# Moving weight-conversion steps and one pair's transposes within an attention stage on one core

## The chip, the cores and the metric

The kernel runs on 1 core of one Trainium2 chip. The metric is the device time of one execution in microseconds, as the median of several runs. All data are fp32; the MLP weights come as 64-bit floats and are converted on the chip.

## What is computed

Softcapped attention, then two MLPs, for 2 batches of 448 tokens, 12 heads of 64:

```python
scores = scale * np.matmul(q, k.transpose(0, 1, 3, 2))
scores = cap * np.tanh(scores / cap)
scores = scores - np.max(scores, axis=-1, keepdims=True)
attn = np.exp(scores)
attn = attn / (np.sum(attn, axis=-1, keepdims=True) + 1e-09)
x = np.matmul(attn, v)                  # then 896 tokens x 768
r = np.maximum(x @ w_in, 0.0)           # w_in 768 x 2048
x = (s * (r * r) + b) @ w_out           # w_out 2048 x 768
h = x @ w2_in                           # 768 x 1024, then softmax-gated,
...
out = ln @ w2_out                       # normalised, and 1024 x 768
```

## The kernel before, in words

Every fp32 product with full precision is made of three matmuls, of a high and a low part each (`xh`, `xl`).

**Attention** works on 12 pairs of heads, counted from 0 (`NPR` is 12); two pairs make a group, and a group's q, k and v are loaded together (`load_group`). For a pair n: `prep` (two halves, called by `prep_half`) transposes keys and queries on TensorE (L426, tiles `pk`, `pq`) and splits them into `kh`, `kl`, `qh`, `ql` on VectorE and ScalarE (L437 to L450). `scores_by_key` makes four blocks of scores (L468) in a ring of two PSUM tiles `s`; ScalarE takes the tanh of each (L473, tile `e`). `exps_by_key` exponentiates in two halves on ScalarE (L480). `sums_by_key` adds the tiles of `e` for the denominator: half 0 is one GpSimd addition (L489), half 1 is another (L492) and then two VectorE additions (L495), all into `c`. `products_by_key` multiplies with the values on TensorE (L507, tile `o`), `values_by_key` sums `c` over the keys on TensorE (L517, tile `m`); VectorE then turns `m` (L524, `mt`), takes reciprocals (L526), turns them back (L530) and scales `o` (L535, `xf`). `split_x` makes the MLP's input from `xf`, on GpSimd (L544, L548) but for the last two pairs. The tiles `pk`, `pq`, `o` and `m` share a ring of four PSUM tiles.

**Order.** The helper `then` traces a step so that each engine issues it behind everything traced by an earlier `then` step. So the order of the calls in the loop over n (L766 on) is the order within each engine. In round n of the loop stand: scores 0 and 1 of pair n, products and values of pair n-2, the first half of the exponentials, scores 2 and 3, the second half, both halves of `prep` of pair n+2, some steps of weight conversion, and last `sums_by_key(n, 1)`. What round 0 has ahead of the loop is scores 0 and 1 of pair 0 and `prep` of pair 1.

**Weight conversion.** `Weights` holds the jobs, one for each weight block, in order: `wi0`, `wi1`, `wi2` and so on. `load` issues a block's DMA on SP's queue into one of two raw buffers (L286); a job loads the next block when it starts. `pump(n)` advances the current job by n steps. The steps of `convert` are: 1, the absolute value (L222 on VectorE for `wi0`, else L226 on ScalarE) and a clamp on VectorE (L227); 2, a shift (L231); 3, an AND and OR with the high word (L236); 4, an OR with the low word (L240), after which the raw buffer is free; 5, the copy to the high part (L247 on VectorE for `wi0`, else L249 on ScalarE) and the subtraction to the low part (L250). A sixth call closes the job. There are three places for converted blocks, so three blocks can be converted before the MLP frees one. The number of steps in each round of the attention loop is in the table `steps`, by round; rounds 12 and 13 have two each besides:

```python
steps = {1: 3, 2: 2, NPR - 2: 2, NPR - 1: 3}
```

**DMA queues.** Keys and values go over SP's queue (L112, L117). The queries of groups 0 (but for its first pair), 1 and 2 go over GpSimd's queue, those of later groups over SP's (L126).

**After attention** the first MLP's first matmuls (`in_unit`, L335 to L337) and ScalarE's relu (L353) and square follow; the conversion of further blocks is pumped between the matmuls.

Of the kernel before, what the change touches and what calls it, by code (L numbers as in the profile page):

```python
# [37 lines left out]
def tile_softcap_attention__relu2__solu(  # L38
# [15 lines left out]
    nc = tc.nc  # L54
# [67 lines left out]
    def load_by_query(t, src, b, heads, eng=None):  # L122

        for pr in range((heads.stop - heads.start) // 2):
            for j in range(2):
                (eng or nc.sync).dma_start(  # L126
                    out=t[:, pr, :, j],
                    in_=src[b, heads.start + 2 * pr + j].rearrange("(p c) d -> p c d", c=NC),
                )
# [11 lines left out]
    for pr in range(2):  # L141
# [3 lines left out]
        if pr == 0:  # L145
            for j, queue in enumerate((nc.sync, nc.scalar)):
                queue.dma_start(
                    out=first["q"][:, 0, :, j],
                    in_=q[0, j].rearrange("(p c) d -> p c d", c=NC),
# [14 lines left out]
    with psum("ps_w", 1) as ps_w:  # L164
# [4 lines left out]
        out=a_t.bitcast(U32), in0=cap_t.bitcast(U32), scalar1=0x7FFFFFFF, scalar2=None,  # L169
# [4 lines left out]
        out=sc_t, in0=r_t, scalar1=1.0 / float(D) ** 0.5, scalar2=None, op0=ALU.mult  # L174
# [7 lines left out]
    def layers(ctx, general):  # L182
# [33 lines left out]
        def convert(wt, raw, n, h, l, g=None, early=False):  # L216
            r = raw[:, :2 * n].rearrange("p (n w) -> p n w", w=2)
            lo, hi = r[:, :, 0], r[:, :, 1]
            w = wt[:, :n]
            wb = w.bitcast(U32)  # L220
            if early:
                nc.vector.tensor_scalar(  # L222
                    out=wb, in0=hi, scalar1=0x7FFFFFFF, scalar2=None, op0=ALU.bitwise_and
                )
            else:
                nc.scalar.activation(out=w, in_=hi.bitcast(F32), func=AF.Abs)  # L226
            nc.vector.tensor_scalar(  # L227
                out=w, in0=w, scalar1=LEAST, scalar2=MOST, op0=ALU.max, op1=ALU.min
            )
            yield  # L230
            nc.vector.tensor_scalar(  # L231
                out=wb, in0=wb, scalar1=3, scalar2=0x3FFFFFFF,
                op0=ALU.logical_shift_left, op1=ALU.bitwise_and,
            )
            yield
            nc.vector.scalar_tensor_tensor(  # L236
                out=wb, in0=hi, scalar=0xC0000000, in1=wb, op0=ALU.bitwise_and, op1=ALU.bitwise_or
            )
            yield
            nc.vector.scalar_tensor_tensor(  # L240
                out=wb, in0=lo, scalar=29, in1=wb,
                op0=ALU.logical_shift_right, op1=ALU.bitwise_or,
            )
            yield
            if g is None:
                if early:
                    nc.vector.tensor_copy(h, w)  # L247
                else:
                    nc.scalar.copy(out=h, in_=w)  # L249
                nc.vector.tensor_tensor(out=l, in0=w, in1=full(h), op=ALU.subtract)  # L250
            else:
                nc.scalar.mul(out=h, in_=w, mul=g)
                nc.vector.scalar_tensor_tensor(
                    out=l, in0=w, scalar=g, in1=full(h), op0=ALU.mult, op1=ALU.subtract
                )
            yield
# [128 lines left out]
        def load_group(g, names=("k", "q", "v")):  # L385
            b, i = divmod(g, GB)
            heads = slice(4 * i, 4 * i + 4)
            for nm, src in (("k", k), ("q", q), ("v", v)):
                if nm not in names:
                    continue  # L390
                by_key = nm != "q" and not general
                if g == 0 and (nm == "q" or nm == "k" and by_key):
                    nat[nm, g] = first[nm]
                    continue
                by_pair = nm != "v"
                shape = [P, 2, NC, 2, D] if by_pair else [P, 4, NC * D]
                if by_key:
                    if (nm, g % 3) not in kept:
                        kept[nm, g % 3] = ap_.tile(shape, F32, name=f"{nm}n{g % 3}")
                        zero_by_key(kept[nm, g % 3], by_pair)  # L400
                    t = kept[nm, g % 3]
                    load_by_key(t, src, b, heads, by_pair)
                    nat[nm, g] = t
                    continue
                t = ap_.tile(shape, F32, tag=f"{nm}n", name=f"{nm}n{g}", bufs=3)
                if by_pair:
                    t = t[:CP]
                    load_by_query(t, src, b, heads, nc.gpsimd if g < 3 else None)
                else:
                    t = t[:CP]  # L410
                    nc.sync.dma_start(out=t, in_=by_query(src, b, heads))
                nat[nm, g] = t
# [296 lines left out]
        NPR = NH // 2  # L709
# [8 lines left out]
        if general:  # L718
            load_group(2, ("v",))
            for n in range(NPR + 2):  # L720
                for c in range(NC):
                    i, c2 = 2 * n + c // 2, c % 2
                    if i < NH:
                        scores(i, c2)
                    if 0 <= i - 1 < NH:
                        exps(i - 1, c2)
                    if 0 <= i - 2 < NH:
                        transposes(i - 2, 2 * c2)
                        transposes(i - 2, 2 * c2 + 1)
                    if c < 2:  # L730
                        prep_half(n + 1)
                if n % 2 == 1 and n // 2 + 3 < NG:
                    load_group(n // 2 + 3)
                if n >= 2:
                    values(n - 2)
        else:
            last = {}
            traced = nc.cur_bb.bb.instructions

            def then(step, *args):  # L740
                with ExitStack() as behind:
                    for ins in last.values():
                        behind.enter_context(tc.issue_after(ins))
                    n = len(traced)
                    step(*args)
                for ins in traced[n:]:
                    if ins.engine in ordered:
                        last[ins.engine] = ins

            ordered = [e.engine for e in (nc.tensor, nc.vector, nc.scalar, nc.gpsimd)]  # L750
            xs["x"] = act_tiles("x")
            idle = ps_t.tile([P, 512], F32, tag="t", name="idle2")
            for n in range(6):
                nc.tensor.matmul(idle[:D, :D], lhsT=ones, rhs=ones, start=True, stop=True)
            then(scores_by_key, 0, 0)
            then(scores_by_key, 0, 1)
            then(prep_half, 1)
            then(prep_half, 1)
            weights.load(0)
            load_group(2, ("k", "q"))  # L760
            load_small()
            load_group(1, ("v",))
            load_group(2, ("v",))
            weights.load(1)
            steps = {1: 3, 2: 2, NPR - 2: 2, NPR - 1: 3}
            for n in range(NPR + 2):  # L766
                now = n < NPR
                if now and n > 0:
                    then(scores_by_key, n, 0)
                    then(scores_by_key, n, 1)  # L770
                if not now:
                    then(weights.pump, 2)
                if n >= 2:
                    then(products_by_key, n - 2, 0)
                    then(products_by_key, n - 2, 1)
                    then(values_by_key, n - 2)
                if now:
                    then(exps_by_key, n, 0)
                if n >= NPR:
                    then(split_x, n - 2)  # L780
                elif n >= 3:
                    then(split_x, n - 3)
                if now:
                    then(sums_by_key, n, 0)
                    then(scores_by_key, n, 2)
                    then(scores_by_key, n, 3)
                    then(exps_by_key, n, 1)
                then(prep_half, n + 2)
                then(prep_half, n + 2)
                then(weights.pump, steps.get(n, 0))  # L790
                if now:
                    then(sums_by_key, n, 1)
                if n == NPR - 1:
                    then(split_x, n - 2)
                if n % 2 == 1 and n // 2 + 3 < NG:
                    load_group(n // 2 + 3, ("k", "q"))
                if n % 2 == 1 and 3 <= (n + 3) // 2 < NG:
                    load_group((n + 3) // 2, ("v",))
# [3 lines left out]
        for n in range(GSB):  # L802
# [3 lines left out]
            if n % 2 == 0:  # L806
# [3 lines left out]
                    out=gl[:, ends], in0=b_t.to_broadcast([P, 2]), in1=full(gh[:, ends]),  # L810
# [299 lines left out]
```

## Time and profile before

| | us |
|---|---|
| median of 3 runs | 480.56 |
| lowest, highest | 479.7, 480.65 |
| the profiled execution | 481.76 |
| its span | 479.9 |

The profile is of one execution. Times of its rows count from the span's start, in us. PE is TensorE, PEld its weight loads, DVE VectorE, ACT ScalarE, POOL GpSimd, SP SyncE; L12 is line 12 of the kernel. A row of a timeline gives start, duration, engine, line, operation, the tiles written and read, the shapes, how many instructions are merged in it, and in brackets the idle time of the engine just before it and what ended it. The granted clock is a share of 2.4 GHz; the two levels are 1.0 and 0.5 (1.2 GHz).

### The profile page before, as it was taken

The page shows a single profiled execution, that of the slowest core. Times are in us where ns is not written, and L with a number is a line of the kernel's source. Part 1 is how long each engine was busy: PE and PEld are TensorE (multiplying, and loading weights), DVE is VectorE, ACT ScalarE, POOL GpSimd, SP SyncE. Part 2 cuts the span into 40 slices and gives each one's busy share as a digit, 9 for nine tenths or more (in the row PEclk, how much of TensorE's full clock was granted, in tenths as well). Part 3 has the DMA queues.
Part 4 walks back from the last instruction along what each step waited for, and adds up shares of the span by engine and source line. Part 5 has one row for each costly group of instructions (what it writes and reads, how often), then busy time and mean ns, then how long its engine had stood idle before and what let it go on. Part 6 is the DMA issues. An engine that isn't in the chain of part 4 may idle for free.

```text
span 479.9 us, 6593 instructions
## 1 busy us (share of the span) xinstructions
PE 462.2 (96%) x2432; PEld 379.4 (79%) x2432; DVE 354.5 (74%) x567; ACT 272.2 (57%) x393; POOL 95.3 (20%) x95
## 2 busy tenths in 40 slices
PE   7796999999899999999999999999999999999995
PEld 6543555545889989989989889989888898999894
DVE  2699888889798899997599998998958984043110
ACT  3895698992296577666577755555535552033120
POOL 8775678785000000000000000000001010000000
PEclk9897999999999999999999999999999999999998
DMA  8975711002445666552132323444312300011112
GB/s 159 187 176 117 177 39 40 0 1 66 141 144 177 185 211 219 197 175 89 45 87 89 102 94 124 139 135 155 132 66 68 131 1 18 16 33 34 34 45 62
DMA packets 43417, 49.28 MB, mean 103 GB/s; under 512 B 20016, under 2 KB 35504, under 8 KB 43376
## 3 DMA queue, kind: packets, MB, share of 16 engines
q1 hardware_dynamic: 41712, 47.39, 34.2%
q0 software_dynamic: 576, 1.15, 1.1%
q8 instruction: 21, 0.34, 0.3%
q10 hardware_dynamic: 1088, 0.23, 0.2%
q14 instruction: 20, 0.16, 0.1%
HBM read 46.01 MB, written 2.75 MB: 102 GB/s over the span
## 4 chain that ended last, share of the span: by engine, by line
PE 83%; DVE 8%; DMA 3%; SPq 3%; issue 1%; ACT 1%; DVEq 0%; ACTq 0%
PE y L337 8%; PE y L336 8%; PE y L335 8%; PE in L335 7%; PE in L337 7%; PE in L336 7%; PE o L507 5%; PE s L468 4%; PE h L980 4%; PE h L984 4%; PE h L988 4%; PE o L1030 4%; PE o L1029 4%; PE o L1031 4%; DVE c L495 2%; SPq L112 2%
## 5 line engine op out<-in xcount | busy, mean ns | idle before, releaser
L335 PE MATMUL in<-xh,h_wi 128*128 128x510 f32 (+2 forms) x192 | 70.1, 366 | 1.2 <-ACT g L353 1.2
L336 PE MATMUL in<-xl,h_wi 128*128 128x510 f32 (+2 forms) x192 | 70.0, 365 | 0.0
L337 PE MATMUL in<-xh,l_wi 128*128 128x510 f32 (+2 forms) x192 | 69.9, 365 | 0.0
L965 POOL TENSOR_SCALAR va<-vs 128x1 f32<-128x1 f32 x7 | 2.0, 286 | 322.3 <-ACT e L964 322.3
L367 ACT ACTIVATE gh<-g,s_t 128x510 fp32r<-128x510 f32 (+1 forms) x64 | 42.0, 669 | 18.4 <-PE y L337 18.3
L473 ACT ACTIVATE e<-s 128x896 f32<-128x896 f32 (+1 forms) x48 | 36.8, 818 | 17.5 <-PE s L468 17.5
L507 PE MATMUL o<-e,vn 128*64 128x448 f32 x192 | 41.6, 576 | 4.1 <-DVE mt L524 4.1
L368 DVE SCALAR_TENSOR_TENSOR gl<-g,s_t,gh 128x510 fp32r<-128x510 f32 (+1 forms) x64 | 42.6, 680 | 2.6 <-ACT gh L367 2.5
L335 PEld LDWEIGHTS in<-xh,h_wi 128*128 128x128 f32 x192 | 36.0, 187 | 6.6 <-ACT g L353 1.6
L480 ACT ACTIVATE e<-e,a_t 128x1792 f32<-128x1792 f32 (+1 forms) x24 | 40.7, 1698 | 0.8
L336 PEld LDWEIGHTS in<-xl,h_wi 128*128 128x128 f32 x192 | 36.0, 188 | 4.3 <-issue 0.7
L337 PEld LDWEIGHTS in<-xh,l_wi 128*128 128x128 f32 x192 | 36.0, 188 | 4.3 <-issue 0.7
L1029 PE MATMUL o<-w2o_h,lh 128*128 128x384 f32 (+1 forms) x104 | 35.6, 342 | 0.5 <-ACT lh L203 0.5
L1031 PE MATMUL o<-w2o_h,ll 128*128 128x384 f32 (+1 forms) x104 | 35.4, 342 | 0.0
L1030 PE MATMUL o<-w2o_l,lh 128*128 128x384 f32 (+1 forms) x104 | 35.4, 340 | 0.0
L495 DVE SCALAR_TENSOR_TENSOR c<-c,e 64x448 f32<-64x448 f32 x24 | 29.8, 1240 | 7.3 <-POOL c L492 6.9
L507 PEld LDWEIGHTS o<-e,vn 128*64 128x64 f32 x192 | 13.9, 144 | 25.9 <-issue 18.9
L980 PE MATMUL h<-w2i_h,yh 128*128 128x512 f32 x84 | 33.0, 393 | 0.0
L984 PE MATMUL h<-w2i_l,yh 128*128 128x512 f32 x84 | 33.0, 392 | 0.0
L988 PE MATMUL h<-w2i_h,yl 128*128 128x512 f32 x84 | 32.8, 390 | 0.0
L489 POOL TENSOR_TENSOR c<-e 128x896 f32<-128x896 f32 x12 | 29.1, 2423 | 4.0 <-ACT e L480 3.8
L492 POOL TENSOR_TENSOR c<-c,e 128x896 f32<-128x896 f32 x12 | 25.7, 2140 | 16.4 <-ACT e L480 16.3
(429 smaller groups left out, 1094.0 us busy)
## 6 DMA issues: line engine op xcount, KB each, us to landing
raw<-in_moe_w_in_dram SPq DMA_DIRECT2D x16, 768.0 KB, 5.1
raw<-in_moe_w_out_dram SPq DMA_DIRECT2D x24, 512.0 KB, 3.6
raw_w2i<-in_moe_w_in_dram SPq DMA_DIRECT2D x12, 512.0 KB, 5.6
raw<-in_moe_w_out_dram SPq DMA_DIRECT2D x8, 768.0 KB, 4.4
vn<-in_v_dram SPq DMA_DIRECT2D x12, 128.0 KB, 2.8
qn<-in_q_dram SPq DMA_DIRECT2D x12, 112.0 KB, 2.8
kn<-in_k_dram SPq DMA_DIRECT2D x20, 64.0 KB, 4.3
vn<-in_v_dram SPq DMA_DIRECT2D x12, 96.0 KB, 2.6
```

The costliest lines, as they stand in the source:

```text
L335: nc.tensor.matmul(o, lhsT=wh, rhs=xh, start=first, stop=False)
L336: nc.tensor.matmul(o, lhsT=wh, rhs=xl, start=False, stop=False)
L337: nc.tensor.matmul(o, lhsT=wl, rhs=xh, start=False, stop=last)
L367: nc.scalar.mul(out=gh[:, :m], in_=r2, mul=s_t)
L368: nc.vector.scalar_tensor_tensor(out=gl[:, :m], in0=r2, scalar=s_t, in1=full(gh[:, :m]), op0=ALU.mult, op1=ALU.subtract,)
L507: nc.tensor.matmul(o[j * D:(j + 1) * D, :S], lhsT=vn[:, 2 * (n % 2) + j, c * D:(c + 1) * D], rhs=st["e", n][:, 2 * c + j if c < 3 else 6, ...
L980: nc.tensor.matmul(ps[:, n, :], lhsT=yh[:, kk, :], rhs=big["w2i_h"][:, kk, f], start=(kk == 0), stop=False,)
L984: nc.tensor.matmul(ps[:, n, :], lhsT=yh[:, kk, :], rhs=big["w2i_l"][:, kk, f], start=False, stop=False,)
L988: nc.tensor.matmul(ps[:, n, :], lhsT=yl[:, kk, :], rhs=big["w2i_h"][:, kk, f], start=False, stop=(kk == KD - 1),)
L1029: nc.tensor.matmul(o, lhsT=lh[:, f, :], rhs=wh, start=(f == 0), stop=False)
L1030: nc.tensor.matmul(o, lhsT=lh[:, f, :], rhs=wl, start=False, stop=False)
L1031: nc.tensor.matmul(o, lhsT=ll[:, f, :], rhs=wh, start=False, stop=(f == KF2 - 1))
```

## The change

It has four parts. The high part of `wi0` is copied by ScalarE, as for the other blocks. The queries of group 2 are loaded over SP's queue. The table of conversion steps loses the two of round 2 and gets one each in rounds 3 to 9. Both halves of `prep` of pair 2 and `sums_by_key(0, 1)` go from the end of round 0 into round 1, behind scores 0 and 1 of pair 1.

```diff
             if g is None:
-                if early:
-                    nc.vector.tensor_copy(h, w)
-                else:
-                    nc.scalar.copy(out=h, in_=w)
+                nc.scalar.copy(out=h, in_=w)
                 nc.vector.tensor_tensor(out=l, in0=w, in1=full(h), op=ALU.subtract)
...
-                    load_by_query(t, src, b, heads, nc.gpsimd if g < 3 else None)
+                    load_by_query(t, src, b, heads, nc.gpsimd if g < 2 else None)
...
-            steps = {1: 3, 2: 2, NPR - 2: 2, NPR - 1: 3}
+            steps = {1: 3, **{n: 1 for n in range(3, NPR - 2)}, NPR - 2: 2, NPR - 1: 3}
             for n in range(NPR + 2):
                 now = n < NPR
                 if now and n > 0:
                     then(scores_by_key, n, 0)
                     then(scores_by_key, n, 1)
                 if not now:
                     then(weights.pump, 2)
+                if n == 1:
+                    then(prep_half, 2)
+                    then(prep_half, 2)
+                    then(sums_by_key, 0, 1)
                 if n >= 2:
...
-                then(prep_half, n + 2)
-                then(prep_half, n + 2)
+                if n > 0:
+                    then(prep_half, n + 2)
+                    then(prep_half, n + 2)
                 then(weights.pump, steps.get(n, 0))
-                if now:
+                if now and n > 0:
                     then(sums_by_key, n, 1)
```

## Rows read from the trace of the kernel before

**Rows 1.** The page: span, and TensorE's busy time, share and instructions.
```profile
span 479.9 us, 6593 instructions
...
PE 462.2 (96%) x2432; PEld 379.4 (79%) x2432; DVE 354.5 (74%) x567; ACT 272.2 (57%) x393; POOL 95.3 (20%) x95
```

**Rows 2.** TensorE's waits, 0 to 150 us: total us, times, longest.
```profile
PE o L507 <- DVE mt L524: 4.1, 2, 3.7
PE pk L426 <- DMA kn<-in_k_dram: 1.9, 1, 1.9
...
PE in L335 <- ACT g L353: 1.2, 1, 1.2
```

**Rows 3.** Busy time by stretch: stretch, length, PE, PEld, DVE, ACT, POOL, PEclk, DMA.
```profile
12.00:24.00 12.00, 8.98 (x56) 6.60 (x52) 8.30 (x13) 10.15 (x10) 8.90 (x12) 0.86 1.17 187
...
44.00:51.75 7.75, 7.75 (x28) 3.42 (x29) 7.24 (x11) 0.47 (x2) 4.20 (x3) 0.65 0.51 122
...
90.50:98.25 7.75, 7.75 (x51) 4.28 (x50) 6.51 (x10) 6.87 (x8) 6.47 (x5) 1.00 0.00 0
```

**Rows 4.** Timeline of TensorE.
```profile
32.44 3.23 PE L507 MATMUL o<-e,vn 128*64 128x448 f32 x16 [0.40 <-DVE mt L524]
...
39.92 0.37 PE L468 MATMUL s<-qh,kl 64*128 64x448 f32 x2
43.97 5.94 PE L507 MATMUL o<-e,vn 128*64 128x448 f32 x16 [3.69 <-DVE mt L524]
...
54.44 3.23 PE L507 MATMUL o<-e,vn 128*64 128x448 f32 x16
...
62.20 3.23 PE L507 MATMUL o<-e,vn 128*64 128x448 f32 x16
```

**Rows 5.** Timeline of VectorE, 21 to 44 us.
```profile
21.44 0.69 DVE L449 CAST kh<-pk 128x512 fp32r<-128x512 f32 x1 [0.77 <-PE pk L426]
...
25.26 2.35 DVE L231 TENSOR_SCALAR wt_wi<-wt_wi 128x768 uint32<-128x768 uint32 x1
...
31.73 0.65 DVE L524 STREAM_TRANSPOSE mt<-m 128x448 f32<-128x448 f32 x1
...
35.83 0.95 DVE L240 SCALAR_TENSOR_TENSOR wt_wi<-raw,wt_wi 128x768 uint32<-128x768 uint32 x1
36.81 2.35 DVE L247 CAST h_wi<-wt_wi 128x768 fp32r<-128x768 f32 x1
39.19 0.96 DVE L250 TENSOR_TENSOR l_wi<-wt_wi,h_wi 128x768 fp32r<-128x768 f32 x1
...
43.27 0.65 DVE L524 STREAM_TRANSPOSE mt<-m 128x448 f32<-128x448 f32 x1
```

**Rows 6.** Timeline of VectorE, 95 to 112 us.
```profile
95.45 2.46 DVE L495 SCALAR_TENSOR_TENSOR c<-c,e 64x448 f32<-64x448 f32 x2 [1.04 <-POOL c L492]
...
101.78 1.81 DVE L227 TENSOR_SCALAR wt_wi<-wt_wi 128x768 f32<-128x768 f32 x1 [1.57 <-ACT wt_wi L226]
...
108.78 2.73 DVE L236 SCALAR_TENSOR_TENSOR wt_wi<-raw,wt_wi 128x768 uint32<-128x768 uint32 x1
```

**Rows 7.** Timeline of GpSimd.
```profile
8.72 2.80 POOL L126 DMA_DIRECT2D qn<-in_q_dram  x4
...
22.02 2.10 POOL L489 TENSOR_TENSOR c<-e 128x896 f32<-128x896 f32 x1 [2.65 <-ACT e L480]
...
101.07 2.10 POOL L492 TENSOR_TENSOR c<-c,e 128x896 f32<-128x896 f32 x1 [1.19 <-ACT e L480]
```

**Rows 8.** Timeline of ScalarE.
```profile
18.19 1.83 ACT L473 ACTIVATE e<-s 128x896 f32<-128x896 f32 x2 [1.75 <-PE s L468]
...
112.77 0.84 ACT L249 CAST h_wi<-wt_wi 128x768 fp32r<-128x768 f32 x1 [4.61 <-DVE wt_wi L240]
...
130.12 0.89 ACT L226 ACTIVATE wt_wi<-raw 128x768 f32<-128x768 f32 x1 [3.61 <-DMA raw<-in_moe_w_in_dram]
```

**Rows 9.** Timeline of SP's queue.
```profile
16.16 4.33 SPq L112 DMA_DIRECT2D kn<-in_k_dram  x6
```

## The prediction

> **What bounds the kernel now.** The page comes first: TensorE is busy for 462.2 of 479.9 us, so the time is what TensorE's matmuls take plus the stretches in which it stands or runs at the lower clock [rows 1]. I therefore looked for those in the first 150 us, the only part that the change touches. TensorE's waits name three that matter here, in all 7.2 us: 4.1 us for `mt` of VectorE, 1.9 us for the keys of group 1, 1.2 us for ScalarE at the start of the first MLP [rows 2]. Busy time by stretch shows the second half of the price, the granted clock: 0.86 over the 12 us from 12 to 24, that is 0.14 x 12 = 1.7 us of full-speed work lost, and 0.65 over the 7.75 us behind the longest wait, 0.35 x 7.75 = 2.7 us lost [rows 3]. Part of each stretch runs at 1.2 GHz instead of 2.4.
>
> The timeline of TensorE places the big wait. The scores of pair 4 (counting from 0) end at 39.92 + 0.37 = 40.29; the products of pair 2, next in its queue, start at 43.97, after 3.69 us. They take 5.94 us where the same 16 matmuls of pair 3 take 3.23. From products to products it is 62.20 - 54.44 = 7.76 us in the undisturbed rhythm, but 54.44 - 43.97 = 10.47 us here: 2.71 us more, the loss that the clock showed too [rows 4].
>
> What `mt` of pair 1 was late for is in VectorE's timeline. Ahead of it stand the last steps of the first weight block: the OR with the low word (0.95 us), the copy to `h_wi` (2.35) and the subtraction to `l_wi` (0.96), together 4.26 us, and `mt` starts at 43.27, ending at 43.92 [rows 5]. Without the 4.26 us it would end near 39.7, before TensorE asks for it at 40.29. After 54 us TensorE no longer waits: in the last stretch shown VectorE is busy 6.51 of 7.75 us [rows 3], and idles 1.04 us a pair ahead of `c`, for GpSimd's sum [rows 6].
>
> **The change part by part.**
> *Steps taken out of pair 2.* Removed there: 4.26 us of VectorE. The wait of 3.69 us at products 2 goes, and with it the 2.71 us of slow rhythm behind it: -6.40 us. I count it in full because `mt` of pair 1 then follows `mt` of pair 0 by 43.27 - 31.73 - 4.26 = 7.28 us, less than TensorE's own 40.29 - 32.44 = 7.85 us between the two products [rows 4, 5]. So even where products 1 still wait for `mt`, products 2 don't.
>
> *The copy to `h_wi`* goes from VectorE to ScalarE, behind pair 4's query scaling. VectorE saves 2.35 us; ScalarE pays some 0.84, as for the second block [rows 8], in a pair in which it is busy 6.87 of 7.75 us [rows 3], so it fits with nothing to spare. Taken at 0; bounds 0 and 0.9.
>
> *The steps put into pairs 3 to 10.* Pair 3 gets the OR, pair 4 the subtraction, pair 5 only the closing of the block; pairs 6 to 9 get one step of the second block each, pair 10 its subtraction, where before the second block began. So six pairs (3, 4, 6 to 9) carry one VectorE operation more. The wait for GpSimd's sum is not free time: the clamp that stood in it at 101.78 lasted 1.81 us, ending at 103.59, 0.42 us after the sum that had begun at 101.07 and ended at 103.17. The worst, the AND-OR at 108.78, lasted 2.73 [rows 6, 7]. A step thus runs its last 0.4 to 0.8 us behind the sum, and `c`, `mt` and the next pair's evacuations come that much later. But the 1.04 us idle of the next pair takes up 0.8 us, so the delay doesn't add up from pair to pair. Taken at 0; bounds 0 and, at 2.73 - 1.04 = 1.7 us over in each of six pairs, 10 us.
>
> The Trainium skill ("SBUF — State Buffer", section "Who interferes with whom") speaks against the change here: GpSimd and a VectorE instruction with two SBUF inputs, or in a two-port mode, share a port pair under an exclusive lock, and the later one stands for the whole of the other's instruction. The 1.81 us row agrees. By that rule alone the filled wait gives VectorE nothing, and the sum would differ by the last rival below.
>
> *Third pair's transposes behind the second's first scores.* Behind pair 0's scores TensorE stands 1.9 us for `kn`, with the scores of pair 1 queued behind that wait [rows 2]. ScalarE stands 1.75 us, until 18.19, for those scores [rows 8]. Moved ahead, they can start once ScalarE has emptied a bank, so ScalarE and the work that it releases run about 1.75 us earlier, up to 2.1 (my estimate) with the slow clock of that stretch gone. That would be the gain, were it TensorE's path. But products 1, which already wait 0.40 us for `mt` of pair 0 at 32.44 [rows 4], depend on VectorE, whose work ahead of that `mt` is unchanged: four conversion steps, one of them stretched to 2.35 us by GpSimd [rows 5]. `mt` of pair 0 can come as much as 2.1 us earlier. It can also come later: GpSimd's first sum of pair 1 moves from 22.02 to near 19.9, where pair 0's two `c` additions stand in VectorE's queue; one of them may wait out that sum's 2.10 us, less the 0.77 us that VectorE idles there now: 1.3 us later [rows 5, 7]. I take no shift: the 1.75 us become wait ahead of products 1, now some 2.1 us long. Would the clock fall again? The nearest row is that wait of 1.9 us for `kn`, behind which 1.7 us were lost [rows 2, 3]; bounds 0 and 2.7 (the wait of 3.69 us). Taken: +1.7 us.
>
> *Group 2's queries from GpSimd's queue to SP's.* GpSimd's queue loses four issues, 2.80 us [rows 7]; its first sum can start earlier, and less is in flight while group 1's keys land. SP's queue gets four issues behind group 2's keys, which delays the values of groups 1 and 2 and the second weight block by some 2.9 us, at 4.33/6 an issue [rows 9]; none of these is needed so early. Pair 4's transposes need the first queries some 2 us ahead of products 1, near 28 us, and the keys' issues end near 20.5. 0; bounds 0 and 2.
>
> *The end of attention.* At 130.12 ScalarE takes up the fifth block's first step, after 3.61 us of waiting for its load, and the emptying of TensorE's bank stands behind it: 1.21 us of TensorE [rows 2, 8]. With the third block converted before the MLP, its raw buffer comes free earlier and the load lands earlier: -1.2 us; bounds -1.2 and 0.
>
> **Sum:** -6.40 + 1.7 - 1.2 = -5.9 us. The profiled execution took 481.76 us (span 479.9 plus 1.86 around it), 1.2 us above the median of 480.56; it would come to 475.9, the median to **474.7**.
>
> **The rivals.**
> *All of the early shift arrives.* `mt` of pair 0 comes 2.1 us earlier as well, with no new wait and no slow clock: -6.40 - 2.1 - 1.2 = -9.7, 470.9 us. For it: less contended loads. Against it: the collisions with GpSimd. 0.22.
>
> *The wait comes back whole, one pair earlier.* The early sums of GpSimd meet `c`, `mt` of pair 0 is 1.3 us late, and the wait ahead of products 1 passes 3 us with the full slow stretch: -6.40 + 1.3 + 2.7 - 1.2 = -3.6, 477.0 us; 478.2 if the end of attention gains nothing. For it: the c additions have two inputs in SBUF, as the operations that rows 6 show stretched. Against it: one lucky order of two starts is enough to avoid it. 0.16.
>
> *Slower: the steps meet GpSimd's additions in pairs 3 to 9.* If each costs the 2.73 us of the AND-OR row, each of the six pairs runs 1.7 us over and TensorE waits for `mt`: +10.2 - 7.6 = +2.6, 483.2 us. It decides once a step costs 1.04 + 7.6/6 = 2.3 us. Against it: one step a pair, and the row of 1.81 us shows only 0.42 behind the sum. 0.08.
>
> *No change.* The queries on SP's queue come late for pair 4, and TensorE stands near 28 us for what it gains at 40, some 6 us: 480.6. 0.04.
>
> **How the numbers follow.** The forecast has 0.50. The range goes from the first rival with 0.2 us more to the second's end with half a microsecond of step cost: 470.7 to 478.7. A measurement of this kernel tells about 0.2% from no change, 1 us. Faster by more: 0.50 + 0.22 + 0.16 = 0.88; same 0.04; slower 0.08.
>
> **What would show it.** Right: products 2 with no wait, period near 7.76 from there; products 1 with a wait of 1 to 3 us for `mt`; a clock below 1 around 32 to 36 us and full at 44; `c` with no idle time ahead of it in pairs 3, 4 and 6 to 9; no ScalarE wait for a load near 130 us. Wrong: TensorE waiting for `mt` in pairs 5 to 9, for `qn` near 28 us, or products 2 still waiting.

## The result and the profile after

The changed kernel takes 475.38 us (median of 4 runs, 474.39 to 477.94) against 480.61 us (4 runs); the ratio is 0.9899, 95% interval 0.9855 to 0.9944. The profiled execution took 475.96 us, with a span of 474.2 us against 479.9. The profiled executions thus lie 5.8 us apart and the medians 5.2, since the profile before is of an execution 1.2 us above its median and the one after of one 0.6 above. From the lines that the change removed up to the loop over n, every line number is 3 lower: L504 is the old L507, L521 the old L524, L492 the old L495, L489 and L486 the GpSimd sums, L465 the scores.

The page, first the span and the busy time, which answer to [rows 1]:

```profile
span 474.2 us, 6582 instructions
...
PE 458.5 (97%) x2432; PEld 378.1 (80%) x2432; DVE 358.2 (76%) x566; ACT 273.1 (58%) x394; POOL 92.5 (20%) x91
```

TensorE's waits, 0 to 150 us, as in [rows 2]:

```profile
PE o L504 <- DVE mt L521: 3.5, 5, 1.3
PE s L465 <- ACT e L470: 2.9, 4, 1.4
...
PE in L332 <- ACT xh L203: 0.4, 1, 0.4
```

Busy time by stretch, columns as in [rows 3]:

```profile
12.00:24.00 12.00, 9.30 (x66) 6.08 (x64) 9.07 (x14) 11.90 (x12) 8.07 (x6) 1.00 0.75 171
...
36.00:48.00 12.00, 11.35 (x78) 6.95 (x78) 11.70 (x14) 10.98 (x13) 9.40 (x6) 1.00 0.45 101
```

The wait for keys is gone, and the clock (the third number from the right) is at 1.00 in both stretches. The wait for `mt` has not gone: 4.1 us in two pieces became 3.5 us in five. TensorE's timeline shows where they stand; it answers to [rows 4] and begins with the products of pair 0:

```profile
14.47 0.47 PE L465 MATMUL s<-qh,kh 64*128 64x448 f32 x2 [1.35 <-ACT e L470]
...
22.19 3.23 PE L504 MATMUL o<-e,vn 128*64 128x448 f32 x16
...
31.29 3.23 PE L504 MATMUL o<-e,vn 128*64 128x448 f32 x16 [1.27 <-DVE mt L521]
...
39.05 3.23 PE L504 MATMUL o<-e,vn 128*64 128x448 f32 x16
...
47.52 3.23 PE L504 MATMUL o<-e,vn 128*64 128x448 f32 x16 [0.65 <-DVE mt L521]
...
55.72 3.23 PE L504 MATMUL o<-e,vn 128*64 128x448 f32 x16 [0.37 <-DVE mt L521]
...
71.72 3.30 PE L504 MATMUL o<-e,vn 128*64 128x448 f32 x16 [0.42 <-DVE mt L521]
...
88.19 3.30 PE L504 MATMUL o<-e,vn 128*64 128x448 f32 x16 [0.80 <-DVE mt L521]
```

The `o` rows are the products of pairs 0, 1, 2, 3, 4, 6 and 8. In the kernel before, the products of pairs 0 and 8 are:

```profile
24.21 3.23 PE L507 MATMUL o<-e,vn 128*64 128x448 f32 x16
...
93.21 3.23 PE L507 MATMUL o<-e,vn 128*64 128x448 f32 x16
```

An account of the span follows:

| | before | after | difference |
|---|---|---|---|
| start of products 1 | 32.44 | 31.29 | -1.15 |
| products 1 to products 2 | 11.53 | 7.76 | -3.77 |
| products 2 to products 8 | 49.24 | 49.14 | -0.10 |
| products 8 to the end of the span | 386.7 | 386.0 | -0.7 |
| span | 479.9 | 474.2 | -5.7 |

The third line hides two things. Before, its first interval was 10.47 us and the other five 7.75; so 2.71 us of slow rhythm went. What came in their place is 49.14 - 6 x 7.76 = 2.58 us of new waits for `mt`.

VectorE's timeline, round 3, the first with a spread step:

```profile
41.88 0.95 DVE L240 SCALAR_TENSOR_TENSOR wt_wi<-raw,wt_wi 128x768 uint32<-128x768 uint32 x1
42.74 4.05 DVE L492 SCALAR_TENSOR_TENSOR c<-c,e 64x448 f32<-64x448 f32 x2
46.82 0.65 DVE L521 STREAM_TRANSPOSE mt<-m 128x448 f32<-128x448 f32 x1
```

and GpSimd's beside it:

```profile
39.16 2.10 POOL L489 TENSOR_TENSOR c<-c,e 128x896 f32<-128x896 f32 x1 [1.90 <-ACT e L477]
...
41.88 1.97 POOL L545 TENSOR_TENSOR xl<-xf,xh 128x448 fp32r<-128x448 f32 x1
43.80 2.50 POOL L486 TENSOR_TENSOR c<-e 128x896 f32<-128x896 f32 x1
```

The sum that `c` needs ends at 41.26, before the step starts at 41.88. There is no wait left to fill: VectorE comes late by itself, and its two additions into `c`, 2.46 us together in [rows 6], stretch over GpSimd's next operations to 4.05 us. `mt` follows at 46.82, and products 3 wait for it. In the kernel before, the same round has no idle time ahead of `c` either:

```profile
47.36 3.03 DVE L495 SCALAR_TENSOR_TENSOR c<-c,e 64x448 f32<-64x448 f32 x2
```

The 1.04 us are there only from the next round on.

### The profile page after: what moved, and what is told of

The parts are those of the page before. It is cut to its first block, busy times and chain, and to the rows that moved or that the text cites. A ratio compares the mean times of both kernels' runs of the same rounds, so it can differ in the third digit from the quotient of the medians.

```text
span 474.2 us, 6582 instructions
## 1 busy us (share of the span) xinstructions
PE 458.5 (97%) x2432; PEld 378.1 (80%) x2432; DVE 358.2 (76%) x566; ACT 273.1 (58%) x394; POOL 92.5 (20%) x91
## 3 DMA queue, kind: packets, MB, share of 16 engines
HBM read 46.01 MB, written 2.75 MB: 103 GB/s over the span
## 4 chain that ended last, share of the span: by engine, by line
PE 75%; DVE 16%; SPq 4%; DMA 2%; issue 1%; ACT 1%; ACTq 0%; DVEq 0%
PE y L333 8%; PE y L334 8%; PE y L332 8%; PE in L332 7%; PE in L333 7%; PE in L334 7%; DVE c L492 5%; PE h L982 4%; PE h L986 4%; PE h L990 4%; PE o L1032 4%; PE o L1033 4%; PE o L1031 4%; SPq L112 3%; PE o L504 1%
## 5 line engine op out<-in xcount | busy, mean ns | idle before, releaser
L504 PE MATMUL o<-e,vn 128*64 128x448 f32 x192 | 39.0, 545 | 3.5 <-DVE mt L521 3.5
L492 DVE SCALAR_TENSOR_TENSOR c<-c,e 64x448 f32<-64x448 f32 x24 | 33.1, 1377 | 0.4
L504 PEld LDWEIGHTS o<-e,vn 128*64 128x64 f32 x192 | 13.7, 136 | 23.4 <-issue 16.8
L486 POOL TENSOR_TENSOR c<-e 128x896 f32<-128x896 f32 x12 | 28.9, 2406 | 5.7 <-ACT e L477 5.3
L489 POOL TENSOR_TENSOR c<-c,e 128x896 f32<-128x896 f32 x12 | 25.6, 2130 | 14.2 <-ACT e L477 14.2
```

Source lines behind the costliest of these rows:

```text
L492: nc.vector.scalar_tensor_tensor(out=c[r, j, :], in0=c[r, j, :], scalar=1e-9 / D, in1=e[r, 6, :], op0=ALU.add, op1=ALU.add,)
L504: nc.tensor.matmul(o[j * D:(j + 1) * D, :S], lhsT=vn[:, 2 * (n % 2) + j, c * D:(c + 1) * D], rhs=st["e", n][:, 2 * c + j if c < 3 else 6, ...
```

## The experiments

Each ran beside the kernel before on one chip, in three groups on three chips: the old table to no middle steps, then the four with fewer early steps or one more instruction, then the copy and the last three. A ratio is to the kernel before on the same chip; medians of different groups are not compared closely. Since an execution's first 24 us differ by up to 1.7 us for a cause of their own (last section), the measure here is the time from the start of products 0 to that of products 8 ("0 to 8"), and inside it 2 to 8. Before: 69.00 and 49.24. Changed: 66.00 and 49.14.

### The old table of steps

```diff
-            steps = {1: 3, **{n: 1 for n in range(3, NPR - 2)}, NPR - 2: 2, NPR - 1: 3}
+            steps = {1: 3, 2: 2, NPR - 2: 2, NPR - 1: 3}
```

> The changed kernel with the old table of steps (two steps in round 2, none in rounds 3 to 9). Theory A (the wait at products 2 was VectorE's lateness, and the steps put into pairs 3, 4 and 6 to 9 cost TensorE 2.7 us because they leave VectorE late): TensorE waits again at products 2, but only 1 to 2 us, since the copy is now ScalarE's and all begins about 1.2 us earlier; no fall of the clock; then 7.76 us a pair with no further wait, so the last products start within 1 us of the changed kernel's 101.02; at the end of attention about 1 us is lost for want of the third block. Span 474 to 476. Theory B (the spread of the steps is what brings the gain): products 2 wait 3 us or more, the clock falls, span 478 or more.

Measured: 478.55 us, ratio 0.9938 (0.9916 to 0.9959), span 476.9; 0 to 8 takes 67.10 us. Neither theory was right about the place: products 2 don't wait at all. ScalarE's timeline has the cause, and TensorE's the wait, now at the scores of pair 3.

```profile
36.49 0.83 ACT L246 CAST h_wi<-wt_wi 128x768 fp32r<-128x768 f32 x1 [5.20 <-DVE wt_wi L240]
37.23 1.72 ACT L470 ACTIVATE e<-s 128x896 f32<-128x896 f32 x2
```

```profile
38.19 0.47 PE L465 MATMUL s<-qh,kh 64*128 64x448 f32 x2 [2.10 <-ACT e L470]
...
39.00 0.73 PE L465 MATMUL s<-qh,kh 128*128 128x448 f32 x1
```

The copy, now ScalarE's, stands in ScalarE's queue ahead of pair 3's tanh and waits there for VectorE's OR step of the same round. TensorE waits 2.10 us for the tanh, the granted clock is 0.50 (1.2 GHz) from 39.04 to 42.45 us (the score matmul there takes 0.73 us instead of 0.47), and then there is no wait for `mt` in any pair. So the copy on ScalarE waits when it stands in the round of its OR step; a round later, as the new table has it, it doesn't. In these surroundings the new table is worth 1.1 us of 0 to 8, far from the 6.40 that taking the steps out of pair 2 was put at: against the kernel without middle steps (63.34 us, below) taking them out gains 3.8 us, and putting them into rounds 3 to 9 gives 2.7 of these back.

### The transposes back at the end of round 0

```diff
-                if n == 1:
-                    then(prep_half, 2)
-                    then(prep_half, 2)
-                    then(sums_by_key, 0, 1)
...
-                if n > 0:
-                    then(prep_half, n + 2)
-                    then(prep_half, n + 2)
+                then(prep_half, n + 2)
+                then(prep_half, n + 2)
...
-                if now and n > 0:
+                if now:
                     then(sums_by_key, n, 1)
```

> The changed kernel with pair 2's transposes and the second sum of pair 0 back at the end of round 0. Theory A (the moved transposes give ScalarE 1.7 us and TensorE's clock its start): keys of group 1 land near 15 us or at best near 14, TensorE waits for them ahead of pair 1's scores, ScalarE stands 1 to 2 us; products 0 start near 24 instead of 22.19, products 1 near 32.4 instead of 31.29; if the wait is as long as before, the clock falls once near 15 us. Span 475 to 476. Theory B (the queue move alone brings the keys early enough): no wait for keys, products 0 near 22.2 and products 1 near 31.3, span as changed, 474.2.

Measured: 476.27 us, ratio 0.9904 (0.9874 to 0.9933), span 473.7; 0 to 8 takes 65.65 us. Theory B in the times, though not without a wait: with the queries off GpSimd's queue TensorE waits 0.76 us for the keys, until 13.85 (1.9 us in the kernel before), inside the 1.35 us that the changed kernel waits there for ScalarE anyway. Products 0 start at 22.15, against 22.19.

```profile
13.85 0.66 PE L423 MATMUL pk<-ident,kn 128*128 128x128 f32 x4 [0.76 <-DMA kn<-in_k_dram]
```

### Group 2's queries back on GpSimd's queue

```diff
-                    load_by_query(t, src, b, heads, nc.gpsimd if g < 2 else None)
+                    load_by_query(t, src, b, heads, nc.gpsimd if g < 3 else None)
```

> The changed kernel with group 2's queries on GpSimd's queue again. Theory A (the queue move matters only through GpSimd's own start): GpSimd's first sum starts near 15.1 instead of 13.76, the second ends near 19.3 instead of 18.66, and pair 0's additions on VectorE move by 0.1 us, so that one of them meets the next sum near 20.0: products 1 0 to 1.5 us later than 31.29, span 474 to 476. Theory B (the keys of group 1 need the freed transfers): pair 2's transposes wait for keys behind pair 1's scores, 15.89 becomes 16.5 or more, and products 1 come 1 us or more later.

Measured: 477.28 us, ratio 0.9923 (0.9902 to 0.9945), span 475.4; 0 to 8 takes 66.07 us, products 0 to 1 9.07 us against 9.10. TensorE's only waits between 12 and 24 us are those for ScalarE, as in the changed kernel; none for keys. The span is longer by what the start cost in this execution: products 0 are at 23.32, behind a stretch at the lower clock (granted 0.50 from 7.84 to 11.25 us) that begins ahead of everything edited. So the moved transposes and the moved queue do the same thing twice: the first alone takes the wait for keys off TensorE, the second alone leaves 0.76 us of it, which costs nothing.

### No steps in rounds 2 to 9

```diff
-            steps = {1: 3, **{n: 1 for n in range(3, NPR - 2)}, NPR - 2: 2, NPR - 1: 3}
+            steps = {1: 3, NPR - 2: 2, NPR - 1: 3}
```

> The changed kernel with no conversion step in rounds 2 to 9, so only one block and most of the second are converted before the MLP. Theory A (the steps in pairs 3 to 9 cost 2.7 us of TensorE's waits): products 2 at 39.05, then 7.76 us a pair with no wait for mt: products 8 at 85.6 instead of 88.19, last products at 98.4 to 99; the MLP's first matmuls wait for the second and third block, which gives back 1 to 5 us. Theory B (the waits for mt in pairs 3 to 8 come from the lateness taken over from products 1 and not from the steps): waits for mt remain at products 3 to 8, 1 us or more in all.

Measured: 474.98 us, ratio 0.9871 (0.9845 to 0.9898), span 472.8; 0 to 8 takes 63.34 us, 2 to 8 46.52. TensorE's timeline from products 1 on, and VectorE's in rounds 4 and 8:

```profile
32.41 3.23 PE L504 MATMUL o<-e,vn 128*64 128x448 f32 x16 [1.22 <-DVE mt L521]
...
40.18 3.23 PE L504 MATMUL o<-e,vn 128*64 128x448 f32 x16
...
86.70 3.23 PE L504 MATMUL o<-e,vn 128*64 128x448 f32 x16
```

```profile
50.19 2.46 DVE L492 SCALAR_TENSOR_TENSOR c<-c,e 64x448 f32<-64x448 f32 x2 [0.87 <-POOL c L489]
...
81.19 2.47 DVE L492 SCALAR_TENSOR_TENSOR c<-c,e 64x448 f32<-64x448 f32 x2 [1.04 <-POOL c L489]
```

After products 1 nothing waits for `mt`, and VectorE has its idle time again, from round 4 on as in the kernel before. In round 3, which has no step here, `c` takes 2.10 us and has no idle time ahead of it. Theory A: the spread steps cost 49.14 - 46.52 = 2.62 us, all of the new waits. The feared loss at the MLP didn't come: from products 8 to the 200th matmul of the first MLP it is 63.92 us, against 64.00 with the spread steps.

### Fewer steps early: one in round 1, and none

These edits are shown against the kernel without middle steps.

```diff
-            steps = {1: 3, NPR - 2: 2, NPR - 1: 3}
+            steps = {1: 1, NPR - 2: 3, NPR - 1: 3}
```

> No steps in rounds 2 to 9, and one instead of three in round 1; three and three in rounds 10 and 11. Theory A (the 1.2 us that TensorE waits ahead of products 1 come from the conversion steps of round 1 on VectorE): no wait at products 1, so products 0 to products 1 take 7.76 us instead of 9.05; nothing else changes up to pair 8; the end of attention carries three steps more in rounds 10 to 13 and loses 0 to 1 us. About 1.2 us below the run with no middle steps, 473.8. Theory B (the late conversion is what the end of attention waits for): what is gained at products 1 is lost as waits between pair 9 and the first MLP matmuls, 475 or more.

```diff
-            steps = {1: 3, NPR - 2: 2, NPR - 1: 3}
+            steps = {NPR - 2: 4, NPR - 1: 4}
```

> No steps before round 10, four each in rounds 10 and 11. Theory A: as with one step in round 1, 473.5 to 474; VectorE has 2 us a pair to spare from round 10 on, where no pair is prepared any more. Theory B: rounds 10 and 11 get too full, mt of pairs 8 to 10 comes late, TensorE waits 1 us or more ahead of products 9 to 11 or at the first matmuls of the second block.

Measured: 478.17 us, ratio 0.9953 (0.9935 to 0.9971), and 476.77 us, ratio 0.9924 (0.9907 to 0.9942). Theory A holds up to pair 8: products 0 to 1 take 7.76 us in both, 0 to 8 62.04, so the wait at products 1 comes from the conversion in round 1. Theory B holds behind it: from products 8 to the 200th matmul of the MLP 69.4 us in both, 5.4 more than above. With one step early, TensorE's timeline and VectorE's in round 10:

```profile
104.10 0.97 PE L514 MATMUL m<-c,ones 128*64 128x448 f32 x2 [1.46 <-DVE c L492]
...
116.72 0.48 PE L332 MATMUL in<-xh,h_wi 128*128 128x448 f32 x1 [1.25 <-ACT xh L203]
...
119.11 0.47 PE L332 MATMUL in<-xh,h_wi 128*128 128x448 f32 x1 [1.05 <-ACT h_wi L246]
```

```profile
94.86 1.26 DVE L231 TENSOR_SCALAR wt_wi<-wt_wi 128x768 uint32<-128x768 uint32 x1
96.15 1.19 DVE L236 SCALAR_TENSOR_TENSOR wt_wi<-raw,wt_wi 128x768 uint32<-128x768 uint32 x1
97.38 1.80 DVE L240 SCALAR_TENSOR_TENSOR wt_wi<-raw,wt_wi 128x768 uint32<-128x768 uint32 x1
99.10 4.94 DVE L492 SCALAR_TENSOR_TENSOR c<-c,e 64x448 f32<-64x448 f32 x2
```

Three steps (4.3 us with GpSimd between them) ahead of `c` are too much for round 10. Behind the waits of 1.25 and 1.05 us, with 0.18 us between them, the granted clock is 0.50 from 119.61 to 123.02 us.

### What a step costs: one more instruction in place of the steps

To the kernel without middle steps a helper is added, called behind the steps of rounds 3, 4 and 6 to 9; it works on scratch tiles, whose making is left out here, as are the calls.

```diff
+            def extra():
+                nc.vector.scalar_tensor_tensor(
+                    out=scr[1].bitcast(U32), in0=scr[0].bitcast(U32), scalar=29,
+                    in1=scr[1].bitcast(U32), op0=ALU.logical_shift_right, op1=ALU.bitwise_or,
+                )
```

> The run with no middle steps, with one more VectorE instruction at the step's place in rounds 3, 4 and 6 to 9: a shift and OR of two scratch tiles in SBUF, 0.95 us by the row of the OR step. It computes nothing that is used. Theory A (the steps cost because they and the additions into c take turns with GpSimd): products 2 to products 8 take 48.5 to 50 us instead of 46.52, with waits for mt, and the additions into c take 3.1 to 4.2 us a pair instead of 2.46. Theory B (it is not the instruction but the state that it belongs to, the raw buffer's loads or ScalarE's part): 46.5 to 47.

```diff
+            def extra():
+                nc.vector.transpose(out=scr[1], in_=scr[0])
```

> The same with a transpose of a 128x640 scratch tile, one SBUF input, 0.92 us by the rows of the 448-wide transposes. It computes nothing that is used. Theory A (turns with GpSimd are the cost): it runs through in the wait for GpSimd's sum, the additions into c start when that sum ends as before, products 2 to products 8 take 46.5 to 47 us. Theory B (VectorE's own time is the cost): as long as with two inputs, 48.5 to 50 us.

Measured: with two inputs 480.07 us, ratio 0.999 (0.9974 to 1.0006), 2 to 8 49.47 us; with one input 478.26 us, ratio 0.9945 (0.9927 to 0.9964), 2 to 8 46.97. Both lose 3 us more behind products 8. Part of that is the queue of ScalarE again (with one input, its copy waits 3.08 us for VectorE in round 10, and TensorE 1.32 us for the tanh behind it); the rest wasn't followed up. 2 to 8 is what they were made for. The first does what the real steps do. The second costs 0.45 us where the first costs 2.95, as theory A has it, but not for its reason. VectorE, round 7, first with two inputs, then with one:

```profile
75.46 0.95 DVE L752 SCALAR_TENSOR_TENSOR scr<-scr,scr 128x768 uint32<-128x768 uint32 x1
76.32 3.19 DVE L492 SCALAR_TENSOR_TENSOR c<-c,e 64x448 f32<-64x448 f32 x2
```

```profile
75.18 0.83 DVE L752 STREAM_TRANSPOSE scr<-scr 128x640 f32<-128x640 f32 x1
75.94 3.03 DVE L492 SCALAR_TENSOR_TENSOR c<-c,e 64x448 f32<-64x448 f32 x2
```

In both the additions into `c` take 3.0 to 3.2 us instead of 2.46, and neither kernel leaves VectorE idle. A step costs its own time and 0.6 to 0.7 us by which `c` runs into GpSimd's next sum. 6.6 us of work, plus 0.83 and 0.6, make 7.9 to 8.0 us a round in the trace, plus 0.95 and 0.7 make 8.2, against TensorE's 7.76. The two instructions differ in their length too, so whether the inputs matter is not shown by this pair.

### The copy back on VectorE

```diff
-                nc.scalar.copy(out=h, in_=w)
+                if early:
+                    nc.vector.tensor_copy(h, w)
+                else:
+                    nc.scalar.copy(out=h, in_=w)
```

> The changed kernel with the copy to the high part of the first block on VectorE again, in round 4. Theory A (VectorE has no time left in rounds 3 to 9, so each of its instructions shows): 0.55 us alone or up to 2.5 if it meets a GpSimd sum, products 4 or 5 that much later than 47.52 + 8.20, span 475 to 477. Theory B (ScalarE is as full and the copy costs there what it costs here): no change, 474 to 474.5.

Measured: 475.43 us, ratio 0.9903 (0.988 to 0.9926), span 473.9; 0 to 8 takes 64.96 us. Both theories missed: products 4 come 0.45 us later after products 3 (8.64 us against 8.19), and then no product waits at all, pairs 5 to 8 taking 7.75 each. VectorE and GpSimd in round 8, with the kernel before's line numbers:

```profile
81.63 1.61 DVE L236 SCALAR_TENSOR_TENSOR wt_wi<-raw,wt_wi 128x768 uint32<-128x768 uint32 x1
83.16 2.47 DVE L495 SCALAR_TENSOR_TENSOR c<-c,e 64x448 f32<-64x448 f32 x2
```

```profile
80.31 2.11 POOL L492 TENSOR_TENSOR c<-c,e 128x896 f32<-128x896 f32 x1 [0.84 <-ACT e L480]
```

Here the step does what the forecast said: it stands while GpSimd's sum runs to 82.42, ends 0.8 us behind it, `c` takes 2.47 us, and the next round takes up the delay. In the changed kernel the same step of the same round takes 1.47 us and `c` 3.18, and products 8 wait 0.80. The difference that the traces show is whether VectorE reached the round on time: its step starts 1.4 us after products 7 here and 3.3 us after them in the changed kernel. It was made in round 6, by the order of two starts 0.02 us apart. Here VectorE's second addition into `c` starts just ahead of GpSimd's next sum, in the changed kernel just behind it:

```profile
69.60 0.62 DVE L495 SCALAR_TENSOR_TENSOR c<-c,e 64x448 f32<-64x448 f32 x1
69.62 2.58 POOL L489 TENSOR_TENSOR c<-e 128x896 f32<-128x896 f32 x1 [0.53 <-ACT e L480]
```

```profile
68.41 2.58 DVE L492 SCALAR_TENSOR_TENSOR c<-c,e 64x448 f32<-64x448 f32 x1
68.39 2.11 POOL L486 TENSOR_TENSOR c<-e 128x896 f32<-128x896 f32 x1 [0.49 <-ACT e L477]
```

The addition takes 0.62 us in one and 2.58 in the other, and from there on VectorE is on time in the first. Why it came to round 6 in this order, the copy or chance, isn't shown by one profile.

### The third step alone in round 6, beside two kernels once more

The edit is shown against the kernel without middle steps.

```diff
-            steps = {1: 3, NPR - 2: 2, NPR - 1: 3}
+            steps = {1: 2, 6: 1, NPR - 2: 2, NPR - 1: 3}
```

> The run with no middle steps, but with two steps instead of three in round 1 and the third, the AND-OR, alone in round 6; rounds 10 to 13 as there. Theory A (a step costs its own 0.95 us and some 0.7 us by which the additions into c run into GpSimd's next sum, against 1.04 us of idle time a pair; a single one leaves VectorE 0.6 us late, which the lead of some 2.4 us at mt covers): no wait at products 1 nor at products 6 to 8, 1.2 us less from products 0 to products 8 than with no middle steps, the end of attention the same; median 1 us below that kernel on this chip. Theory B (any step in the middle costs TensorE 0.4 us or more): a wait at products 6 or 7, gain 0.8 us or less. Theory C (the place of the late steps sets the end of attention): 1 to 3 us lost after the last products.

> The run with no middle steps once more, beside the changed kernel on one chip. If the steps in rounds 3 to 9 are a pure cost of 2.6 us: 1.5 to 3 us below the changed kernel; if the spread of earlier readings was chance of the start, equal within 1 us.

> The changed kernel once more: 475 to 476.5, ratio to the kernel before 0.988 to 0.992. The intervals between products as in its first profile, whatever the clock does near 10 us.

| | us | ratio (95%) | 0 to 8 | 2 to 8 |
|---|---|---|---|---|
| third step in round 6 | 473.29 | 0.9853 (0.983 to 0.9877) | 63.43 | 47.48 |
| no middle steps | 473.96 | 0.9867 (0.9844 to 0.989) | 63.37 | 46.53 |
| changed | 476.43 | 0.9919 (0.9898 to 0.994) | 65.96 | 49.12 |

TensorE, with the third step in round 6:

```profile
30.51 3.23 PE L504 MATMUL o<-e,vn 128*64 128x448 f32 x16 [0.35 <-DVE mt L521]
...
70.16 3.30 PE L504 MATMUL o<-e,vn 128*64 128x448 f32 x16 [0.81 <-DVE mt L521]
```

Theory B: what is won at products 1, 0.9 us, is lost at products 6. VectorE never got its idle time back between rounds 2 and 6, though no step stands in rounds 2 to 5: `c` took 3.1 to 4.1 us in each, running into GpSimd's sum, and the rounds took 7.24, 8.18, 7.74 and 7.77 us, on average as long as TensorE's. So this is the price of a step in a round without idle time; in a round that has it, this step wasn't tried. In the two profiles the lead of this kernel over the one without middle steps lies in the start (products 0 at 22.32 and at 23.68), not in 0 to 8; where the 0.7 us between the two medians lie isn't shown. The gap between no middle steps and the changed kernel is 2.5 us, with intervals that don't touch: both versions beat the changed kernel, one by leaving out the steps in rounds 3 to 9, the other by keeping a single one.

## Why the prediction was right, and where it was wrong

475.38 us lies 0.7 us above the forecast of 474.7 and inside the range, and the forecast case is the one that came: faster, with a wait left ahead of products 1. But the sum came out by two errors of opposite sign, -2.85 and +2.58 us; that they cancel is luck. Of its own signs, products 2 without a wait and products 1 with a wait of 1 to 3 us came. The clock below 1 around 32 to 36 us didn't (the granted clock is 1.00 from 24 to 48 us), and one of its signs of being wrong did: TensorE waits for `mt` at products 6 and 8. By its terms, against the account of the span:

- **Steps out of pair 2, -6.40 us: right.** Products 2 start without a wait, 7.76 us after products 1, and the slow rhythm behind it is gone: -3.77 - 2.71 = -6.48. `mt` of pair 1 follows `mt` of pair 0 by 7.19 us, forecast 7.28. What the forecast missed is that the old table together with the new copy loses its time on ScalarE instead, and less of it: there the same steps cost 3.8 us.
- **The moved wait and the clock, +1.7 us: wrong.** The step that failed is "I take no shift". `mt` of pair 0 came 1.14 us earlier, so the wait was 1.27 us and not 2.1, products 1 gained 1.15 us, and the clock never fell. (Products 0 came 2.02 us earlier; 0.87 of these became wait.) The collision feared at `c` of pair 0 didn't happen; VectorE took up its third pair at 20.52 instead of 21.44 and kept that through the four conversion steps, although two of these were stretched by GpSimd (2.23 and 2.75 us) instead of one. The term should have been -1.15. This compares two profiles that start alike (the twelve matmuls of the last section take 0.91 us in both); in the changed kernel's second profile, with the slower start, products 1 come at 32.20.
- **The spread steps, taken at 0: wrong, 2.6 us.** The step that failed is "the 1.04 us idle of the next pair takes up 0.8 us". It was read off rounds from 95 us on, in which VectorE is on time. In rounds 2 and 3 there is no such time, in the kernel before no more than in the changed one; VectorE comes to them late. Without middle steps it is back in round 4, though the stretch at the lower clock is gone there too. With a step in round 3 `c` falls on GpSimd's next operations (4.05 us against 2.10 without it), the steps of rounds 4 and 6 to 9 find VectorE late again, and the idle time never comes back. The bounds of 0 to 10 us held it. The kernel with the copy on VectorE shows, in round 8, that the mechanism as forecast exists: it needs VectorE to be on time.
- **The transposes and the queue, 0 us each: right only in the sum.** Either of them alone takes away the cost of the wait for keys; together they do it once.
- **The copy to ScalarE, 0 us: not settled by one number.** 0 to 8 is 1.04 us shorter with the copy on VectorE, and the medians on one chip are 475.43 us against 476.43. In the one profile this comes with the order of two starts in round 6, not with the copy's own time, 0.55 us.
- **End of attention, -1.2 us: the wait is gone, its worth and its cause stay open.** ScalarE's wait for a load is still there, 4.16 us up to 116.87, but ends before TensorE's bank must be emptied; a wait of 0.37 us for `xh` is left. Behind products 8 this profile is 0.7 us shorter than the one before. The changed kernel's second profile isn't: it takes 386.9 us there. The reason given, the third block converted before the MLP, isn't shown: the kernel without middle steps has fewer blocks converted by then, and there the wait of 1.2 us is gone as well (386.1 us).

So -1.15 - 6.48 + 2.58 - 0.7 = -5.75, the -5.7 of the span. Of the rivals, the slower one had its place and its mechanism (the steps' collisions in pairs 3 to 9) right, at a quarter of its price; the port rule of the Trainium skill ("SBUF — State Buffer", "Who interferes with whom"), that the later of the two engines stands for the whole of the other's instruction, agrees with the stretched rows: 1.97 us for a GpSimd subtraction that takes 1.16 alone, and 2.58 for an addition on VectorE that takes 0.62. (Of the rows that the prediction names with two inputs in SBUF, only the AND-OR has two; the clamp has one.)

## What to carry to other kernels

Idle time ahead of one instruction is slack only while its engine is on time. Look for it in each round that is to take the work, not in one round late in the stage. Work put into a wait also moves what follows the wait; ask whom that will meet, here another engine's next instruction. And when a change has several parts, test each alone: here two did the same thing, and one, the steps put into rounds 3 to 9, cost 2.6 us.

## What the runs showed that was not expected

**When the clock first rises differs from execution to execution.** TensorE's timeline of the changed kernel in its first profile, and in the second:

```profile
7.67 0.91 PE L751 MATMUL idle<-ones 128*64 128x64 f32 x12
8.52 0.47 PE L465 MATMUL s<-qh,kh 64*128 64x448 f32 x2
```

```profile
8.08 1.54 PE L751 MATMUL idle<-ones 128*64 128x64 f32 x12
9.55 0.74 PE L465 MATMUL s<-qh,kh 64*128 64x448 f32 x2
```

The same twelve matmuls take 0.91 or 1.54 us, the first score matmuls 0.47 or 0.74. The trace's first record of the full clock is at 5.62 us in the first profile and at 10.55 in the second. In the profiles of this study products 0 of kernels with the new early order start anywhere from 22.15 to 23.85 us; that is a third of the change's whole gain. The two profiles of the changed kernel are 1.8 us apart in span; 0.94 us of it lie ahead of products 0, and as much behind products 8.

**A wait of 1.27 us, or of 1.35, left the clock alone;** the waits of 1.88 and 3.69 us in the kernel before were followed by the lower level, and so was one of 2.10 us in the kernel with the old table. But with one step in round 1, two waits of 1.25 and 1.05 us close together were followed by it too, and one of 1.46 us alone was not. So the length of the single wait doesn't settle it.

**Two rhythms of VectorE and GpSimd.** With the same work, a round of VectorE takes about 6.6 us of busy time when it is on time and up to 7.8 when it is not, because an addition into `c` falls on GpSimd's next sum. The kernels with one early step and with none show both side by side in rounds 2 to 9, where neither has a step: with none `c` takes 2.47 us behind 1.04 us of idle time, with one it takes 3.6 to 3.8 us and there is no idle time, for eight rounds. TensorE's rhythm is 7.75 us in both, so the slow one costs nothing until work is added to it.
